# A bf16-bit exponential on VectorE for 60 of 1024 score banks, and GpSimd's weight copies and key masks removed

## The chip, the cores and the metric

The kernel runs on one core of one Trainium2 chip. The metric is the device time of one execution in microseconds (us), as a median of executions; lower is better. A trace of one execution is taken by the hardware profiler. Its span, from the first instruction to the last, is about 2 us shorter than the reported time of the same execution. Each execution also has a mean granted TensorE clock (1.0 is full); below I call an execution *clean* when that is 0.997 or more.

## The reference, cut to what matters

Two attention branches over 2048 positions, 16 heads of 28, joined at the end:

```python
def _A_ref(x, wq, wk, wv, wo):            # 16 query heads, one key/value head
    q = (x @ wq).reshape(B, S, H, Dh)...; k = x @ wk; v = x @ wv
    scores = einsum("bhqd,bkd->bhqk", q, k) * Dh ** -0.5
    p = softmax(scores); o = einsum("bhqk,bkd->bhqd", p, v)
    return o... @ wo
def _B_ref(x, wqkv, wo):                  # each position sees itself and 7 earlier ones, 2 apart
    ...
return concatenate([a, b], axis=-1)
```

Branch A dominates: 16 x 2048 x 2048 exponentials. The kernel handles them as 1024 *banks* of 128 keys x 512 queries.

## The kernel before

All work is listed as operations with an engine, a modelled duration, dependencies and a priority. A small list scheduler in the kernel file then lays out one fixed order for each engine. That matters for reading every experiment: *any* edit that changes a duration, a dependency or a priority gives a new order on all engines.

The main loop takes five banks a round, in PSUM slots of three and of two banks. TensorE computes scores (QK), ScalarE takes the exponential of a whole slot into one of seven ring buffers, TensorE multiplies by V (PV) in groups of four banks. In 51 rounds the third bank of a slot goes to VectorE instead (`off`). A "quad" is 64 banks, four heads of one query block, whose PV sums share a PSUM bank.

```python
ERING = 7
OFF_EVERY, OFF_FROM, OFF_TO = 6, 28, 396
...
x = a("act", t_exp(w), lambda e, b0=b0, w=w, n=n: e.activation(
    g.expT[:, n % ERING, 0:w], g.ps[:, 512 * b0:512 * b0 + w], ACT.Exp, scale=SCALE), ...)
for i in range(na):
    where.append((us[i], ("expT", n % ERING), g.expT[:, n % ERING, 512 * i:512 * i + 512], 0))
if off:
    where.append((us[na],) + g.d_exp(b0 + na, slot) + (1,))
while len(where) >= 4 or (where and pos == NU):
    grp, where = where[:4], where[4:]          # a PV group: four banks in the order of the keys
    ...
def d_exp(self, bank, slot):                   # VectorE's recipe: five instructions of 512 elements
    a("dve", ..., ii = max(bank * A2 * F, -127 * F))        # PSUM -> int32
    a("dve", ..., ee = (hi + 127.0) * 128.0)                # exponent bits, int16
    a("dve", ..., uu = (lo + EP * F) * lo)                  # a cubic of the fraction
    a("dve", ..., vv = (lo + ER * F) * ee.bitcast(BF16))
    a("dve", ..., out = (uu + EQ * F * F) * vv)             # bf16
```

(The five calls are shortened to their arithmetic; cuts are marked by dots.) Branch B's matrix products, softmax and weighted sums run beside this, in 16 blocks, mostly on VectorE and on PSUM banks of their own.

## Time and profile before

| | before |
|---|---|
| time, median of 4 executions | 482.71 us (482.48 to 486.05) |
| span of the profiled execution (485.64 us) | 483.8 us |
| ScalarE / VectorE / GpSimd busy | 457.4 / 378.6 / 40.7 us |
| banks on ScalarE / VectorE | 973 / 51 |
| first exponential starts, last ends | 12.27, 474.78 us |

The profiled execution was one of the slower ones; the prediction, which quotes the lines of its profile, argued that from the head's clock.

### The profile page before, as it was taken

To read this page: it belongs to the slowest core of one execution; us is meant where nothing else is said; L and a number is where in the kernel's file an instruction comes from. 1 tells how busy PE (TensorE), PEld (TensorE's weight loads), DVE (VectorE), ACT (ScalarE), POOL (GpSimd) and SP (SyncE) were. 2 spreads that over 40 slices of the span, in tenths; PEclk is the share of its full clock that TensorE was granted. 3 is DMA by queue.
4 is the path that set the end of the run, shared out by engine and by line. 5 is a ranking of instruction groups with operands and counts; after the bars stand their busy time and mean duration, and the time that the engine had idled before them with its cause. 6 is when DMAs were issued, how large, how long until landed. Compare 5 with 4: busy or idle time off the path is not lost.

```text
span 483.8 us, 8734 instructions
## 1 busy us (share of the span) xinstructions
PE 456.6 (94%) x3630; PEld 177.3 (37%) x3630; DVE 378.6 (78%) x703; ACT 457.4 (95%) x431; POOL 40.7 (8%) x71
## 2 busy tenths in 40 slices
PE   8999999999999999999999999998999999998886
PEld 3333343333343443433333333433334343333333
DVE  4325787998869888889878988788968989888673
ACT  3789999999999999999999998999999999999993
POOL 8643000000000000000000000000000000000000
PEclk9699999999999999999999999999999999999999
DMA  7890202020200320002020320002300330102001
GB/s 160 146 230 14 88 11 76 11 77 10 87 11 20 106 80 26 11 1 82 6 95 11 110 85 27 11 11 71 102 11 2 105 105 20 58 30 96 1 1 57
DMA packets 42071, 27.34 MB, mean 57 GB/s; under 512 B 17090, under 2 KB 41968, under 8 KB 42032
## 3 DMA queue, kind: packets, MB, share of 16 engines
q1 hardware_dynamic: 40080, 25.65, 18.5%
q10 hardware_dynamic: 1776, 0.81, 0.7%
q8 instruction: 28, 0.46, 0.4%
q0 software_dynamic: 176, 0.33, 0.2%
q14 instruction: 11, 0.09, 0.1%
HBM read 17.60 MB, written 5.52 MB: 48 GB/s over the span
## 4 chain that ended last, share of the span: by engine, by line
ACT 62%; PE 35%; DVE 1%; DMA 1%; ACTq 0%; issue 0%; DVEq 0%
ACT expT L756 62%; PE ps L740 7%; PE ps L902 6%; PE ps L770 6%; PE ps L738 4%; PE ps L688 2%; PE ps L918 2%; PE ps L830 1%; PE ps L1014 1%; PE ps L615 1%; DMA d_i<-in_A_wq_dram 1%; PE ps L651 1%; PE ps L861 1%; PE ps L1007 1%; PE ps L702 0%; PE ps L380 0%
## 5 line engine op out<-in xcount | busy, mean ns | idle before, releaser
L756 ACT ACTIVATE expT<-ps 128x1024 bf16<-128x1024 f32 (+1 forms) x410 | 450.2, 1223 | 11.6 <-PE ps L740 6.2
L740 PE MATMUL ps<-qT,kT 32*128 32x512 bf16 x734 | 111.3, 388 | 12.4 <-ACT expT L756 9.7
L770 PE MATMUL ps<-expT,v_aug 128*32 128x512 bf16 x973 | 98.7, 393 | 0.1
L738 PE MATMUL ps<-qT,kz 128*128 128x512 bf16 x290 | 84.5, 384 | 8.8 <-ACT expT L756 6.9
L740 PEld LDWEIGHTS ps<-qT,kT 32*128 32x128 bf16 x734 | 27.2, 91 | 82.1 <-ACT expT L756 58.4
L770 PEld LDWEIGHTS ps<-expT,v_aug 128*32 128x32 bf16 x973 | 24.1, 93 | 63.6 <-issue 57.8
L943 DVE TENSOR_TENSOR stage<-qTB,kTB 112x1024 bf16<-112x1024 bf16 x64 | 44.0, 706 | 4.0 <-PE ps L952 4.0
L802 DVE TENSOR_SCALAR d_i<-ps 128x512 int32<-128x512 f32 x51 | 35.3, 692 | 14.3 <-PE ps L740 13.1
L838 POOL COPY rrep<-rden 128x512 bf16<-128x512 bf16 x15 | 12.7, 843 | 399.4 <-DVE rden L836 399.4
L902 PE MATMUL ps<-xT_B,wqkv 128*112 128x512 bf16 (+1 forms) x128 | 43.2, 405 | 0.2 <-DVE qT L711 0.2
L996 DVE TENSOR_TENSOR prod<-Vsh,a_n 128x896 bf16<-128x896 bf16 x64 | 38.1, 626 | 0.0
L807 DVE SCALAR_TENSOR_TENSOR d_u<-d_i 128x512 f32<-128x512 uint16 x51 | 36.0, 706 | 0.0
L809 DVE SCALAR_TENSOR_TENSOR d_v<-d_i,d_e 128x512 f32<-128x512 uint16 x51 | 35.2, 690 | 0.0
L812 DVE SCALAR_TENSOR_TENSOR dexp<-d_u,d_v 128x512 bf16<-128x512 f32 x51 | 34.8, 682 | 0.0
L738 PEld LDWEIGHTS ps<-qT,kz 128*128 128x128 bf16 x290 | 19.3, 99 | 35.2 <-ACT expT L756 28.3
L952 PEld LDWEIGHTS ps<-ones,stage 112*128 112x128 bf16 x512 | 20.9, 96 | 13.4 <-issue 7.9
L952 PE MATMUL ps<-ones,stage 112*128 112x4 bf16 x512 | 25.2, 167 | 0.2 <-DVE qT L711 0.2
L1007 PE MATMUL ps<-ident,padd 128*112 128x128 bf16 x256 | 25.1, 226 | 0.0
L1007 PEld LDWEIGHTS ps<-ident,padd 128*112 128x112 bf16 x256 | 18.9, 129 | 12.3 <-issue 9.4
L902 PEld LDWEIGHTS ps<-xT_B,wqkv 128*112 128x112 bf16 (+1 forms) x128 | 14.3, 127 | 22.1 <-issue 17.2
L805 DVE TENSOR_SCALAR d_e<-d_i 128x512 int16<-128x512 int16 x51 | 21.6, 423 | 0.2
L830 PEld LDWEIGHTS ps<-sel,PV_sb 128*128 128x128 f32 x128 | 18.9, 190 | 5.5 <-issue 3.9
(109 smaller groups left out, 441.3 us busy)
## 6 DMA issues: line engine op xcount, KB each, us to landing
Vsh<-v_scratch SPq DMA_DIRECT2D x16, 896.0 KB, 4.6
v_scratch<-Vst SPq DMA_DIRECT2D x16, 112.0 KB, 1.7
out_dram<-outB SPq DMA_DIRECT2D x16, 112.0 KB, 1.7
out_dram<-outA SPq DMA_DIRECT2D x14, 112.0 KB, 1.8
wqkv<-in_B_wqkv_dram SPq DMA_DIRECT2D x1, 672.0 KB, 4.8
stage<-in_A_x_dram ACTq DMA_DIRECT2D x1, 448.0 KB, 3.5
wo_B<-in_B_wo_dram SPq DMA_DIRECT2D x4, 98.0 KB
wo<-in_A_wo_dram SPq DMA_DIRECT2D x4, 98.0 KB
```

The source lines that it names most:

```text
L738: r = e.matmul(g.bank(b0 + i), g.kz[:, j, 128 * tb:128 * tb + 128], g.qT[:, sc % 2, t, :], start=True, stop=True)
L740: r = e.matmul(g.bank(b0 + i), g.kT[32 * j:32 * j + 32, 128 * tb:128 * tb + 128], g.qT[32 * j:32 * j + 32, sc % 2, t, :], start=True, stop ...
L756: x = a("act", t_exp(w), lambda e, b0=b0, w=w, n=n: e.activation(g.expT[:, n % ERING, 0:w], g.ps[:, 512 * b0:512 * b0 + w], ACT.Exp, scale ...
L770: x = e.matmul(g.bank(PVBANK, p0=32 * j, p1=32 * j + 32), g.v_aug[:, w, tb, :], src, start=tb == 0, stop=tb == 15, tile_position=(0, 32 * j))
L802: a("dve", t_dve_ps(512), lambda e: e.tensor_scalar(out=ii, in0=g.bank(bank), scalar1=A2 * F, scalar2=-127 * F, op0=ALU.mult, op1=ALU.max) ...
L807: a("dve", t_dve_1x(512), lambda e: e.scalar_tensor_tensor(out=uu, in0=lo, scalar=EP * F, in1=lo, op0=ALU.add, op1=ALU.mult), R=[("d_i", h ...
L809: a("dve", t_dve_1x(512), lambda e: e.scalar_tensor_tensor(out=vv, in0=lo, scalar=ER * F, in1=ee.bitcast(BF16), op0=ALU.add, op1=ALU.mult) ...
L902: a("pe", t_mm(512), lambda e, u=u, t=t, kt=kt, w=w: e.matmul(g.bank(u.bank, p1=KC), g.wqkv[64 * (kt // 3):, kt, w * D + KC * t:w * D + KC ...
L943: op = a("dve", t_dve_2x(1024), lambda e, t=t, qv=qv, kv=kv: e.tensor_tensor(out=g.prodT[0:KC, t, :, :], in0=qv, in1=kv, op=ALU.mult), R=R ...
L952: r = e.matmul(g.bank(u.bank, 128).rearrange("p (h w) -> p h w", w=WIN)[:, 4 * t:4 * t + 4, w], g.prodT[0:KC, t, w, :], g.ones4[:, :], sta ...
L996: a("dve", t_dve_2x(2 * D), lambda e, qr=qr, Vv=Vv, av=av: e.tensor_tensor(out=g.prod2[:, 2 * qr:2 * qr + 2, :].rearrange("p w (d h) -> p ...
L1007: a("pe", 0.09, lambda e, u=u, t=t, w=w: e.matmul(g.bank(u.bank, 128, 128 * t, p1=KC), g.padd[:, w, KC * t:KC * t + KC], g.ident[:, :], st ...
```

## The change

The intent: take nine more banks from ScalarE with a cheaper VectorE recipe that works directly on the bits of bf16, and remove GpSimd's weight copies and key masks. Around it, PV groups, softmax layout, head and pace of branch B are rearranged. The scheduler's model changes too: durations marked `Lock` are VectorE operations that the model makes longer while GpSimd works, and the other way round. The diff, cut to its core:

```diff
-OFF_EVERY, OFF_FROM, OFF_TO = 6, 28, 396
-DR = 4
+OFF_AT = {q: (0, 2, 5, 7) for q in range(1, 16)}      # rounds of each quad, 4 x 15 = 60 banks
+DR = 2
...
-            g.kz_ops[c] = [a("gp", 0.8, ...
+            g.kz_ops[c] = [a("dve", Lock(0.29), ...           # masks of the keys
...
-        u = Use(f"V{c}", g.LB)
+        u = Use(f"V{c}", g.LB, spare=160)                     # dummy matmuls beside the narrow V ones
...
+                quads[us[i][:2]][us[i][3]].append((us[i], ("expT", n % ERING), ...))
             if off:
-                where.append((us[na],) + g.d_exp(b0 + na, slot) + (1,))
+                dunits.append((us[na],) + g.d_exp(b0 + na, slot))
+                if len(dunits) == 4:
+                    g.pv_group(dunits, 1)                      # VectorE's banks: a PV group of their own
...
 def d_exp(self, bank, slot):
+            out=xx[...], in0=g.bank(bank), scalar1=-128.0 * A2, scalar2=128.0 * (129 + EOFF), mult, add   # PSUM -> fp32
+        if h:                                                  # once for two banks, 1024 elements
+                out=u, in0=lo, scalar=EP * F, in1=lo, op0=ALU.add, op1=ALU.mult
+                out=v, in0=u, scalar=EQ * F * F, in1=lo, op0=ALU.add, op1=ALU.mult
+                out=out, in0=v, scalar=EL / F ** 3, in1=xx, op0=ALU.mult, op1=ALU.subtract   # int16 = bf16 bits
...
-    B0 = 34.0
-    BSTEP = 25.0
+    B0 = 32.0
+    BSTEP = 24.5
...
-        self.e_t = sb([128, 2, 2, H, WIN], FP32, "e_t")
+        self.e_t = sb([128, 2, 2, WIN, H], FP32, "e_t")
-        a("act", t_act(256), lambda e: e.activation(fl(g.e_t), fl(g.lg2), ACT.Exp, scale=SCALE),
+        a("act", t_act(256), lambda e: e.activation(ew, g.lg2[:, par], ACT.Exp, scale=SCALE),    # writes 64 bytes apart
-                out=g.a_n[:, par, b].rearrange("p w h -> p h w"), in0=g.e_t[:, par, b],
+                out=g.a_n[:, par, b], in0=g.e_t[:, par, b],
```

GpSimd's four copies that permuted the V weights go too: the eviction of V permutes instead, and the weights have their own buffer and an early load.

## The prediction

> **What bounds the kernel now.** I read the page first: busy shares, the slices, the chain, the costliest groups. ScalarE is 95% busy and its slices read 9 from the third to the last but one; the chain that ended last is ScalarE's exponentials for 62% of the span and TensorE for 35%.
>
> ```profile
> span 483.8 us, 8734 instructions
> PE 456.6 (94%) x3630; PEld 177.3 (37%) x3630; DVE 378.6 (78%) x703; ACT 457.4 (95%) x431; POOL 40.7 (8%) x71
> ACT  3789999999999999999999998999999999999993
> PEclk9699999999999999999999999999999999999999
> ACT 62%; PE 35%; DVE 1%; DMA 1%; ACTq 0%; issue 0%; DVEq 0%
> ```
>
> TensorE's 94% is pipelined matmuls plus dummy ones; VectorE at 78% has room. So the kernel is a ScalarE stream with a head and a tail. The groups by shape size that stream, and the VectorE rows show what one offloaded bank costs now:
>
> ```profile
> L756 ACT ACTIVATE expT<-ps 128x1024 bf16<-128x1024 f32 x255 | 258.9, 1065 | 4.9 <-PE ps L770 3.2 <-PE ps L740 1.0 <-PE ps L738 0.2
> L756 ACT ACTIVATE expT<-ps 128x1536 bf16<-128x1536 f32 x154 | 229.2, 1488 | 6.7 <-PE ps L740 5.1 <-PE ps L738 0.9
> ...
> L807 DVE SCALAR_TENSOR_TENSOR d_u<-d_i 128x512 f32<-128x512 uint16 x51 | 36.0, 706 | 0.0
> L802 DVE TENSOR_SCALAR d_i<-ps 128x512 int32<-128x512 f32 x51 | 35.3, 692 | 14.3 <-PE ps L740 13.1 <-PE ps L738 0.7
> L809 DVE SCALAR_TENSOR_TENSOR d_v<-d_i,d_e 128x512 f32<-128x512 uint16 x51 | 35.2, 690 | 0.0
> L812 DVE SCALAR_TENSOR_TENSOR dexp<-d_u,d_v 128x512 bf16<-128x512 f32 x51 | 34.8, 682 | 0.0
> ...
> L805 DVE TENSOR_SCALAR d_e<-d_i 128x512 int16<-128x512 int16 x51 | 21.6, 423 | 0.2
> ...
> L983 DVE TENSOR_TENSOR a_n<-e_t,rs 128x128 bf16<-128x128 f32 x16 | 11.4, 757 | 0.1
> ```
>
> The reader is to see that 51 banks are already off ScalarE (154 x 3 + 255 x 2 + 1 = 973 of 1024 remain), and that in the whole run ScalarE waited only 4.9 + 6.7 = 11.6 us ahead of its exponentials. The timeline of ScalarE says where: the first exponential starts at 12.27 us, the last ends at 474.78. Of the 11.6 us, 0.5 is the first start, about 3.4 us fall between 17 and 33 us, 3.2 us are three stalls at 126, 187 and 295 us, and the rest is crumbs of 0.2 to 0.4 us. The three stalls:
>
> ```profile
> 126.15 25.49 ACT L756 ACTIVATE expT<-ps 128x1024 bf16<-128x1024 f32 x23 [1.04 <-PE ps L770]
> 187.35 11.12 ACT L756 ACTIVATE expT<-ps 128x1024 bf16<-128x1024 f32 x10 [0.54 <-PE ps L770]
> 295.22 16.66 ACT L756 ACTIVATE expT<-ps 128x1024 bf16<-128x1024 f32 x15 [1.62 <-PE ps L770]
> ```
>
> At each, the PV group that should free a buffer of the exponential ring contains one VectorE-made bank: at 293.52 us the last step of that bank begins, 0.68 us long, and the PV group follows at 294.77, while ScalarE is out of ring buffers. The stall of the head is the clock. In 2 us windows:
>
> ```profile
> 14.00:16.00 2.00, 2.00 (x17) 0.76 (x14) 1.18 (x2) 2.00 (x3) 0.94 (x2) 1.00 0.62 111
> 16.00:18.00 2.00, 2.00 (x18) 0.93 (x17) 1.06 (x5) 1.59 (x3) 1.68 (x5) 0.54 0.52 101
> 24.00:26.00 2.00, 2.00 (x13) 0.29 (x13) 0.26 (x1) 1.42 (x1) 1.70 (x4) 0.50 0.98 205
> ```
>
> The third number from the right is the granted clock: half from about 17 to 26 us, right after the narrow V matmuls (28 columns) of 12.6 to 14 us.
>
> **What the Trainium skill says.** (1) "ScalarE: Activation LUTs", section "What ACT_TABLE_LOAD costs": 0.833 ns an element, and back-to-back activations overlap by about 93 ns. The trace agrees: (1488 - 1065) / 512 = 0.826 ns, and the durations, about 488.7 us with the one 512 wide, exceed the busy 450.2 by 38.5 us, 94 ns each for 410. So a bank is worth 0.423 us of ScalarE, whatever its neighbours. (2) "VectorE: DVE Perf Modes", section "The TRN2 errata — SBUF-src ops pay a fixed extra latency per instruction": fp32 two-tensor operations take (N + 151) / 0.96 ns, 691 at 512; the trace's 706, 690 and 682 agree, and at 1024 it gives 1224. (3) "Advanced Engine Details and Errata", section "SBUF Cachelines": accesses that each fall in another 16-byte line are penalised. The trace has one case that fits: a_n writes bf16 32 bytes apart and takes 757 ns, while the subtraction of the same 128 x 128, written densely, takes 283. (4) "TensorE: Matmul & The Clock Gate", section "What's actually happening": too little TensorE activity in a window of about 3.4 us halves the clock, and the window runs freely, so the phase differs by run. That fits the half clock above, and perhaps the spread of the three times, 482.48 and 482.72 against 486.05.
>
> **The change part by part.**
> 1. *Nine more banks on VectorE.* Four in each of 15 quads give 60 instead of 51. The count of exponentials stays 410, but 60 - 51 = 9 shrink from 1536 to 1024: 9 x 0.423 = 3.8 us less ScalarE, all on the bounding stream. Minus 3.8.
> 2. *The VectorE recipe.* Before: 692 + 423 + 706 + 690 + 682 = 3193 ns a bank, 51 banks, 162.8 us. After, a pair of banks: two PSUM reads of 692 and three operations of 1024 elements at 1224, so 5056 ns, 30 pairs, 151.7 us. VectorE does nine more banks in 11 us less. Off the path: worth nothing directly, but it lowers the delay of PSUM evacuations.
> 3. *a_n made dense*, 16 x (757 - 283) = 7.6 us less VectorE, off the path. The price is in ScalarE's softmax exponential of branch B, which now writes fp32 64 bytes apart. If it pays what a_n paid per element, (757 - 283) / 128 = 3.7 ns, that is 256 x 3.7 = 0.95 us more on each of 8 calls, 7.6 us on the bounding engine. If ScalarE pays nothing, 0. No row of before shows ScalarE writing with a stride; I choose 2 us as an estimate between. Plus 2.0.
> 4. *PV groups separated.* Banks of VectorE get PV groups of their own, so no group that frees ring buffers contains one. The 3.2 us of stalls lose their cause; but the groups now take their four columns from different key blocks, which holds some ring buffers about 1.6 exponentials longer of 7, and TensorE, in order, can still stand before an early VectorE group. I take 2.5 us off and put 1.0 us back for new waits. Minus 1.5.
> 5. *GpSimd.* Its four weight copies (about 0.95 us each, at 38 to 42 us) and 16 kz masks (706 ns each) go; the masks take about 0.28 us each on VectorE (the 448-element copy of the same kind took 280 ns), 4.5 us in a head where VectorE is a third busy or less. The V eviction now permutes in its PSUM read: possibly longer than 621 ns, not on the path. Zero.
> 6. *Head.* Dummy matmuls beside the narrow V ones should keep the clock. In this trace the half clock cost some 3 us, but the two fast executions are 3 us below the profiled one (485.64), so I hold that the median of 482.72 does not contain it. The gain is in the spread, zero on the median. The added V-weight load on GpSimd's queue competes with the transposed loads; chunk 1 is needed only after 6 or 7 exponentials. Zero.
> 7. *Tail.* Branch B starts 2 us earlier and steps 24.5 instead of 25 us, 9.5 us earlier at its last block. In the tail VectorE's eviction for B (0.69 us from 478.11) pushes the last normalisation from about 478.4 to 478.71, and B's store is issued last. Minus 0.4.
>
> Sum: 482.7 - 3.8 + 2.0 - 1.5 - 0.4 = 479.0. I shade this to 478.5 because lighter VectorE load should also shave some crumbs of waiting.
>
> **The rivals.** *A floor.* Between first start and last end (462.5 us) ScalarE idles 11.1 us; without idle and with 3.8 us less it needs 447.6. With a head of 12.3 and a tail of 9.0 the span is 468.9; the profiled run's time was 1.84 us over its span, so about 470.7 is the least. A gain of over 2% (below 473.1) needs nearly all waiting gone and no stride penalty. For it: the stalls have nameable causes, and the change addresses two. Against it: a static order always leaves crumbs. I give such a result 472 us. *ScalarE's strided write eats the gain.* For it: a_n's 757 ns. Against: that was a 2-byte write on another engine. Full penalty: 482.7 - 3.8 + 7.6 - 1.9 = 484.6, "within 2%". *VectorE's longer instructions become the bound.* A PSUM read that finds a 1.22 us operation just begun frees its bank up to 0.5 us later than now, and a short exponential gives only 0.97 us. Against: the read goes first in the order, the rounds 0, 2, 5, 7 leave the three long operations to rounds without offload, and VectorE's total falls. If a quarter of 60 reads cost 0.4 us: plus 6, 485. *TensorE stalls on an early VectorE PV group*: one stall of 1 us in each quad would be plus 15, 494; the priorities make it improbable.
>
> **Range and chances.** The sum's spread is mainly the stride (0 to 7.6), the waits (-5 to +5) and the clock's phase (3): 473.5 to 484.0, predicted 478.5. Faster by over 2% needs the floor nearly reached: 0.08. Slower by over 2% (above 492.4) needs a new stall per quad: 0.03. Within 2%: 0.89.
>
> **What would show it right or wrong.** Exponentials 145 x 1536 and 264 x 1024 with unchanged means (step 1); three VectorE operations near 1.22 us, 30 times each, and VectorE near 365 us busy (2); the mean of the B softmax exponential against 455 ns, and a_n near 283 ns (3); waits of exponentials for PV gone or below 1 us (4); clock full from 12 to 30 us (6); last exponential to end below 9 us (7). I am wrong if ScalarE's idle ahead of exponentials rises above 11.6 us, or B's exponential is over 1 us, or the head moves by more than 1 us from 12.27.

## The result, and the profile after

| | before | after |
|---|---|---|
| time, median of 4 executions | 482.71 us | 478.56 us (478.50 to 478.89) |
| ratio | | 0.9899, 95% interval 0.9856 to 0.9943 |

The change is faster by 1.0%, inside the band of 2% that the prediction gave most of its chances. Ratios here are the mean time of one kernel's runs over that of the other's runs of the same rounds; so they are not quite the ratio of the medians. Executions over 1.5% slower than the fastest of the same kernel are left out of the means. The 486.05 of before counts in that mean, though its clock was lost for a while. The page of the changed kernel, first busy times, then two slices and the chain:

```profile
span 476.5 us, 8559 instructions
PE 451.4 (95%) x3605; PEld 178.3 (37%) x3605; DVE 375.6 (79%) x614; ACT 454.6 (95%) x431; POOL 29.4 (6%) x45
ACT  3899999999999999999999999999999999999993
PEclk9999999999999999999999999999999999999999
ACT 65%; PE 31%; SPq 1%; DMA 1%; DVE 1%; issue 0%; DVEq 0%
```

Nothing has changed places: ScalarE still reads 9 nearly throughout, and VectorE is almost as busy as before (375.6 against 378.6), although it does nine more banks. The groups of the changed kernel (instructions, shapes, count, then busy us and mean ns, then idle ahead of them and its releasers):

```profile
L766 ACT ACTIVATE expT<-ps 128x1024 bf16<-128x1024 f32 x264 | 264.9, 1047 | 2.7 <-PE ps L750 2.0 <-PE ps L748 0.4
L766 ACT ACTIVATE expT<-ps 128x1536 bf16<-128x1536 f32 x145 | 213.3, 1471 | 4.5 <-PE ps L750 2.5 <-PE ps L748 1.4
L1001 ACT ACTIVATE e_t<-lg 128x256 f32<-128x256 f32 x8 | 5.2, 648 | 0.0
...
L823 DVE TENSOR_SCALAR d_x<-ps 128x512 f32<-128x512 f32 x60 | 41.4, 689 | 11.3 <-PE ps L750 7.4 <-PE ps L748 2.6
L830 DVE SCALAR_TENSOR_TENSOR d_u<-d_x 128x1024 f32<-128x1024 uint16 x30 | 36.5, 1217 | 0.1
L834 DVE SCALAR_TENSOR_TENSOR dexp<-d_u,d_x 128x1024 int16<-128x1024 f32 x30 | 36.4, 1214 | 0.1
L832 DVE SCALAR_TENSOR_TENSOR d_u<-d_u,d_x 128x1024 f32<-128x1024 f32 x30 | 36.3, 1211 | 0.1
L645 DVE TENSOR_SCALAR kz<-kT,cols 128x512 bf16<-128x512 bf16 x16 | 6.3, 391 | 0.4
L1007 DVE TENSOR_TENSOR a_n<-e_t,rs 128x128 bf16<-128x128 f32 x16 | 4.1, 285 | 0.1
```

The counts are 145 and 264 as planned. Releasers named "L770", the PV matmuls that cost 3.2 us of ScalarE before, have no counterpart here (PV is now L790, and it does not appear). The price of the layout is in the third row: 648 ns where 455 stood.

To compare like with like, I ran the kernel before once more.

### x0_before: the kernel before again, for a trace at full clock

No edit.

> The kernel before, unedited, once more for a second trace. Theory (the profiled execution of before had a half clock from 17 to 26 us that its faster executions did not have): if this execution takes about 482.7 us, its trace shows full clock from 12 to 40 us and about 8 us of ScalarE idle ahead of exponentials instead of 11.6; if it takes about 486, the half clock is there again. Rival (the half clock is in every execution, and the 3 us come from elsewhere): half clock at 482.7 us too.

It took 482.63 us, correct. Its trace, the same two windows as in the prediction (third number from the right: clock) and its exponentials:

```profile
16.00:18.00 2.00, 2.00 (x22) 1.10 (x20) 1.40 (x5) 2.00 (x4) 1.68 (x4) 1.00 0.43 89
24.00:26.00 2.00, 2.00 (x20) 0.90 (x20) 0.00 (x0) 2.00 (x4) 0.95 (x2) 1.00 1.14 233
```

```profile
L756 ACT ACTIVATE expT<-ps 128x1024 bf16<-128x1024 f32 x255 | 259.0, 1066 | 4.6 <-PE ps L770 3.2 <-PE ps L740 0.8 <-PE ps L738 0.2
L756 ACT ACTIVATE expT<-ps 128x1536 bf16<-128x1536 f32 x154 | 229.2, 1489 | 4.1 <-PE ps L740 2.5 <-PE ps L738 0.9
```

The clock is full, the idle is 4.6 + 4.1 = 8.7 instead of 11.6 us, and the span is 480.8. So the half clock of the first trace belongs to the slower executions. The three stalls on PV stand unchanged: they belong to the order, not to the clock.

Now the 4.3 us between the spans 480.8 and 476.5 can be split. First exponential: 12.60 against 12.67, nothing. From there to the end of the last: 459.1 against 455.1, minus 4.0. Tail: 9.1 against 8.8, minus 0.3. Within the stretch, all exponentials together occupy 449.7 us of ScalarE before (450.2 in the trace with the half clock) and 446.1 after, minus 3.6; the softmax of B costs 3.6 and 5.2, plus 1.6; the waits inside the stretch (8.7 less 0.5 at the first start, 7.2 less 0.8) fall by 1.8. That is minus 3.8, within a few tenths of the 4.0: records of ScalarE overlap, so such sums are good to that.

### The profile page after: what moved, and what is told of

It is laid out like the page before. It is cut to its first block, busy times and chain, and to the rows that moved or that the text cites.

```text
span 476.5 us, 8559 instructions
## 1 busy us (share of the span) xinstructions
PE 451.4 (95%) x3605; PEld 178.3 (37%) x3605; DVE 375.6 (79%) x614; ACT 454.6 (95%) x431; POOL 29.4 (6%) x45
## 4 chain that ended last, share of the span: by engine, by line
ACT 65%; PE 31%; SPq 1%; DMA 1%; DVE 1%; issue 0%; DVEq 0%
ACT expT L766 64%; PE ps L750 7%; PE ps L924 6%; PE ps L790 5%; PE ps L748 4%; PE ps L852 2%; PE ps L696 2%; PE ps L940 1%; SPq L560 1%; DMA xT_A<-in_A_x_dram 1%; PE ps L883 1%; PE ps L1038 1%; PE ps L660 1%; PE ps L392 1%; ACT e_t L1001 0%
## 5 line engine op out<-in xcount | busy, mean ns | idle before, releaser
L766 ACT ACTIVATE expT<-ps 128x1024 bf16<-128x1024 f32 (+1 forms) x410 | 446.1, 1196 | 7.2 <-PE ps L750 4.5
L748 PE MATMUL ps<-qT,kz 128*128 128x512 bf16 x305 | 88.1, 382 | 9.6 <-ACT expT L766 7.5
L790 PE MATMUL ps<-expT,v_aug 128*32 128x512 bf16 x964 | 95.7, 389 | 0.4
L823 DVE TENSOR_SCALAR d_x<-ps 128x512 f32<-128x512 f32 x60 | 41.4, 689 | 11.3 <-PE ps L750 7.4
L790 PEld LDWEIGHTS ps<-expT,v_aug 128*32 128x32 bf16 x964 | 24.4, 92 | 66.3 <-issue 62.3
L860 POOL COPY rrep<-rden 128x512 bf16<-128x512 bf16 x15 | 16.8, 1122 | 393.8 <-DVE rden L858 393.8
L830 DVE SCALAR_TENSOR_TENSOR d_u<-d_x 128x1024 f32<-128x1024 uint16 x30 | 36.5, 1217 | 0.1
L834 DVE SCALAR_TENSOR_TENSOR dexp<-d_u,d_x 128x1024 int16<-128x1024 f32 x30 | 36.4, 1214 | 0.1
L832 DVE SCALAR_TENSOR_TENSOR d_u<-d_u,d_x 128x1024 f32<-128x1024 f32 x30 | 36.3, 1211 | 0.1
L1031 PE MATMUL ps<-ident,prod 128*112 128x128 bf16 x256 | 25.6, 226 | 0.0
L1031 PEld LDWEIGHTS ps<-ident,prod 128*112 128x112 bf16 x256 | 19.3, 129 | 12.1 <-issue 8.6
L696 PE MATMUL ps<-xT_A,wq 128*128 128x512 bf16 x64 | 20.5, 384 | 0.5 <-DVE v_aug L675 0.3
```

Of the source, the lines that this page charges most:

```text
L748: r = e.matmul(g.bank(b0 + i), g.kz[:, j, 128 * tb:128 * tb + 128], g.qT[:, sc % 2, t, :], start=True, stop=True)
L790: x = e.matmul(g.bank(PVBANK, p0=32 * j, p1=32 * j + 32), g.v_aug[:, w, tb, :], src, start=first, stop=last, tile_position=(0, 32 * j))
L823: a("dve", t_dve_ps(512), lambda e: e.tensor_scalar(out=xx[:, 512 * h:512 * h + 512], in0=g.bank(bank), scalar1=-128.0 * A2, scalar2=128.0 ...
L830: a("dve", t_dve_1x(1024), lambda e: e.scalar_tensor_tensor(out=u, in0=lo, scalar=EP * F, in1=lo, op0=ALU.add, op1=ALU.mult), R=di, W=["d_ ...
L834: a("dve", t_dve_1x(1024), lambda e: e.scalar_tensor_tensor(out=out, in0=v, scalar=EL / F ** 3, in1=xx, op0=ALU.mult, op1=ALU.subtract), R ...
L1031: a("pe", 0.09, lambda e, u=u, t=t, w=w: e.matmul(g.bank(u.bank, 128, 128 * t, p1=KC), g.padd[:, w, KC * t:KC * t + KC], g.ident[:, :], st ...
```

## The experiments

All executions, in us. Numbers in brackets count clean executions. The runs were taken in three groups on three chips; the medians of the kernel before in them were 482.81, 482.70 and 482.77, so runs of different groups may be compared to about 0.2 us.

| run | median | clean executions | ratio to before |
|---|---|---|---|
| changed kernel, first | 478.56 | 478.50 to 478.89 (4 of 4) | 0.9899 |
| a_again, the same | 479.16 | 478.59 to 479.47 (4 of 6) | 0.9914 |
| e1_dense | 478.60 | 477.85 to 478.67 (4 of 6) | 0.9893 |
| e2_48 | 483.80 | 482.70 (1 of 4) | 1.0021 |
| e3_nofill | 480.17 | 478.90, 478.97 (2 of 6) | 0.9944 |
| e6_oldrecipe | 503.87 | none (6) | 1.0404 |
| e7_mixed | 505.06 | none (7) | 1.0431 |
| e8_64 | 480.69 | 480.14 to 481.70 (5 of 6) | 0.9942 |
| e9_old48 | 485.04 | 484.99 to 485.06 (3 of 4) | 1.0036 |
| e12_mixed48 | 501.73 | 500.89, 502.10 (2 of 4) | 1.0400 |
| e10_oldlayout | 477.83 | 477.64 to 478.25 (5 of 6) | 0.9888 |
| e11_bstep | 480.15 | 479.44 to 480.35 (4 of 6) | 0.9951 |

All gave correct results.

### a_again: the control

No edit.

> The changed kernel unedited, as a control for this group of runs. Every theory: fast executions 478.5 to 478.9 as before; the question is only how often the clock is lost (0 of 4 executions so far, against 3 of 11 above 486 for the kernel before on this chip).

Clean executions as before, but two of six lost the clock (486.16 at clock 0.981, 483.60 at 0.985). On the same chip the kernel before lost it in 4 of 11 (485.86 to 486.47, all at 0.989). So the changed kernel is not immune. With its four first executions that is 2 of 10 against 8 of 33 over the three groups of runs: no difference can be claimed.

### e3_nofill: without the dummy matmuls of the head

```diff
-        u = Use(f"V{c}", g.LB, spare=160)
+        u = Use(f"V{c}", g.LB)
```

> The changed kernel without the dummy matmuls beside the narrow V matmuls of the head. Theory (they only keep the clock, whose loss depends on the phase of the execution): most executions about 478.6, some 3 us longer, and a half clock between 16 and 28 us only in the long ones. Rival A (without them every execution loses the clock): all about 481.5. Rival B (they do nothing): all within 0.5 us of 478.6, full clock.

The two clean executions are 0.3 us above the changed kernel's typical time; the other four are 1 to 6 us longer than these, at clocks of 0.982 to 0.996. In the profiled one (479.75 us) the clock was full from 10 to 32 us. It was lost at the other end, in the window of the tail:

```profile
470.00:478.00 8.00, 3.65 (x26) 1.80 (x22) 2.59 (x6) 1.64 (x3) 0.00 (x0) 0.76 0.18 57
```

That loss does not explain this execution's time: its tail (from the last exponential to the end) took 8.4 us, less than the 8.8 of the changed kernel, while its first exponential started 1.1 us later (13.73 against 12.67) at full clock. Other traces end on a half clock too, x0_before for example from 479.6 us on. So neither the theory nor rival A is confirmed; for the clock of the head, this one trace looks like rival B (they do nothing). Since the edit re-laid the whole order, whether the dummy matmuls protect the head stays open.

### e2_48: fewer banks, and e8_64: more

```diff
-OFF_AT = {q: (0, 2, 5, 7) for q in range(1, 16)}
+OFF_AT = {q: (0, 2, 5, 7) for q in range(1, 13)}                                  # e2_48
+OFF_AT = {q: (0, 2, 5, 7) if q else (4, 6, 9, 11) for q in range(16)}             # e8_64
```

> The changed kernel with 12 quads offloaded instead of 15: 48 banks instead of 60. Theory (a bank is worth 0.423 us of the bounding ScalarE): 12 x 0.423 = 5.1 us slower, 483.6. Rival (part of the worth of a bank is lost in waits caused by VectorE's reads and its own PV groups): under 3.5 us slower, at most 482, with ScalarE's idle smaller than 7.2 us.

> The changed kernel with the first quad offloaded too, its rounds 4, 6, 9 and 11: 64 banks. Theory (each bank is worth 0.423 us of ScalarE, less a sixth lost in waits as in the run with 48 banks, where 12 banks made 4.2 us at full clock): 1.4 us below the changed kernel, 477.1. Rival (VectorE or TensorE is loaded in the first quad, with the transposes and projections of the head): no gain, 478.6 or more, with more idle in ScalarE between 17 and 40 us.

With 48 banks the only clean execution took 482.70, some 4.0 us above the control's middle of 478.7. That is 4.0 / 12 = 0.33 us a bank: between the theory's 0.423 and its rival, and from a single clean execution. The profiled execution (484.32, not clean) agrees: its first exponential came 1.5 us later (14.21), but from there to the end of the last, at full clock, it took 459.4 us against 455.1, which is 0.36 a bank. So a bank is worth most of its ScalarE time, not all. Note that 48 banks with the rest of the change take the 482.7 that 51 took before.

With 64 banks the four additional ones made it *slower*, 480.4 against 478.7. The rival holds. ScalarE's own timeline of that run shows where (in brackets at the end: idle ahead of the row and what ended it):

```profile
36.10 5.37 ACT L766 ACTIVATE expT<-ps 128x1024 bf16<-128x1024 f32 x5 [2.00 <-PE ps L750]
...
44.15 9.34 ACT L766 ACTIVATE expT<-ps 128x1024 bf16<-128x1024 f32 x9 [1.26 <-PE ps L790]
```

Two new stalls, 2.00 and 1.26 us, in or just after the first quad, where head work still runs on TensorE and VectorE, outweigh 4 x 0.423 = 1.7. In the changed kernel no stall between 30 and 50 us is longer than 0.27. It fits that the change leaves that quad out.

### e1_dense: the strided write of ScalarE undone

```diff
-        self.e_t = sb([128, 2, 2, WIN, H], FP32, "e_t")
+        self.e_t = sb([128, 2, 2, H, WIN], FP32, "e_t")
-        ew = g.e_t[:, par].rearrange("p b w h -> p b h w")
+        ew = g.e_t[:, par]
-                out=g.a_n[:, par, b], in0=g.e_t[:, par, b],
+                out=g.a_n[:, par, b], in0=g.e_t[:, par, b].rearrange("p h w -> p w h"),
```

The modelled durations are untouched, and the orders of all engines are row for row the same as in the changed kernel (55 records of matmuls are missing from this trace, as they are from a_again's), which makes this the cleanest of the comparisons.

> The changed kernel with branch B's exponential writing densely again, and the normalisation reading it with a stride instead and still writing densely. Theory (the strided fp32 write costs ScalarE 648 - 455 = 0.19 us in each of 8 calls, all on the bounding engine): that exponential back to about 455 ns, total 477.0, 1.5 us below the changed kernel; normalisation on VectorE between 285 and 757 ns, without effect on the total. Rival (the 0.19 us hide in waits): no change, 478.5.

```profile
L766 ACT ACTIVATE expT<-ps 128x1024 bf16<-128x1024 f32 x264 | 265.4, 1049 | 3.0 <-PE ps L750 2.0 <-PE ps L748 0.7
L766 ACT ACTIVATE expT<-ps 128x1536 bf16<-128x1536 f32 x145 | 213.5, 1472 | 5.0 <-PE ps L750 2.9 <-PE ps L748 1.7
L1001 ACT ACTIVATE e_t<-lg 128x256 f32<-128x256 f32 x8 | 3.4, 427 | 0.0
```

The write is back to 427 ns, 8 x (648 - 427) = 1.8 us less. The clean executions gained only about 0.4 (median 478.36 against the control's 478.8; the two ranges overlap). The traces show where the rest went. ScalarE's busy time fell by 1.0 only (454.6 to 453.6), since its records overlap their neighbours. Between the first exponential and the end of the last, the waits ahead of exponentials rose by 0.5 (6.4 to 6.9), and the stretch became 0.6 shorter (455.1 to 454.5). So part of the saving was overlapped before and part is spent waiting for the next scores: the rival is nearer the truth, and "on the bounding engine" does not mean "one for one in the time".

### e6_oldrecipe and e9_old48: the old recipe on the new frame

The five-instruction recipe of before replaces the new one in the changed kernel; the buffers and the constant of the second V weights follow.

```diff
-        xx, out = g.d_x[:, m % 2, :], g.dexp[:, m % DR, :]      # two banks, then three operations of 1024
...
+        h = m % 2                                               # d_exp as in the kernel before
...
+OFF_AT = {q: (0, 2, 5, 7) for q in range(1, 13)}                # e9_old48 in addition
```

> The changed kernel with the old VectorE recipe (five instructions of 512 elements for each bank) on the new 60 banks, with the new PV groups. Theory (VectorE is not the bound, so its cheaper recipe is worth nothing directly): within 0.7 us of the changed kernel, VectorE some 10 us busier. Rival (the recipe's saving is what lets VectorE keep up with 60 banks): over 2 us slower, with more ScalarE idle ahead of exponentials than 7.2 us.

> The old VectorE recipe with new PV groups, at 48 banks instead of 60. Theory (60 banks at 3.19 us each overfilled VectorE, and branch B finished about 25 us late; 48 banks do not overfill it): the last output eviction of branch B returns from 498.7 us to before 480, total 482.7 to 485, within 1.5 us of the run with 48 banks and the new recipe. Rival (the old recipe is slow for another reason, such as its short instructions breaking up the others): more than 5 us above that run.

With 60 banks: 503.87, 25 us slower. This is the largest surprise. VectorE's share on the page is still modest:

```profile
PE 459.5 (92%) x3604; PEld 183.9 (37%) x3658; DVE 403.0 (80%) x764; ACT 456.3 (91%) x431; POOL 24.8 (5%) x45
```

But the exponentials are not what ends late: in e6 the last one is done at 469.2, and ScalarE's idle ahead of them is 7.5 us against 7.2, so the rival's total came, but not by way of ScalarE. Branch B is late. The row of branch B's output evictions (min/median/max ns, then first and last start in us), for the kernel before (the trace of x0_before), the changed one, e6 and e9:

```profile
L1017 DVE CAST outB<-ps x16: 610/624/626, 115.9 to 477.6; 128x448 bf16<-128x448 f32 x16
```

```profile
L1041 DVE CAST outB<-ps x16: 616/625/626, 113.3 to 473.4; 128x448 bf16<-128x448 f32 x16
```

```profile
L1042 DVE CAST outB<-ps x16: 623/625/626, 135.4 to 498.7; 128x448 bf16<-128x448 f32 x16
```

```profile
L1042 DVE CAST outB<-ps x16: 614/625/626, 135.8 to 480.2; 128x448 bf16<-128x448 f32 x16
```

In e6 the first block of B is evicted 22 us later than in the changed kernel and the seventh 60 us later (334.6 against 274.5 us), and the last starts 25 us later. The run with 48 banks has the same times as e6 up to the tenth block (397 against 404), and then, when its last quads offload nothing, catches up: last eviction at 480.2, total 485.0. That is 2.3 us above the 48-bank run with the new recipe, more than the 1.5 I allowed and far less than the rival's 5. My reading: VectorE's time per quad is short. In windows of 100 us between 50 and 350 us it is busy for 81 to 89 us in all these kernels (82 to 86 in the changed one, 84 to 88 in e6), and part of what is left are waits that a fixed order does not fill. The old recipe's 3.19 us a bank, 28.7 us more for nine banks, does not fit in time for branch B; the new recipe's does. That the recipe costs 25 us in the schedule made for it is shown. How much of it is sheer time, and how much a worse order that the scheduler laid out, I did not separate, so the cause is in part argued.

### e7_mixed and e12_mixed48: PV groups that mix both kinds of banks

```diff
-                dunits.append((us[na],) + g.d_exp(b0 + na, slot))
-                if len(dunits) == 4:
-                    g.pv_group(dunits, 1)
...
+                dunits.append((us[i], ("expT", n % ERING), ..., 0))      # ScalarE's banks join the same list
...
+                dunits.append((us[na],) + g.d_exp(b0 + na, slot) + (1,))
+            while len(dunits) >= 4:                 # groups of four in the order of the keys
+                g.pv_group(dunits[:4])
```

on top of e6 and of e9.

> The same as the run with the old recipe, but PV groups formed in the order of the keys again, so that a group that frees exponential buffers may contain one VectorE bank. Theory (these mixed groups cause the stalls of 1.04, 0.54 and 1.62 us of the kernel before): ScalarE's idle that ends on a PV matmul comes back, 2 to 4 us, and the total is 1.5 to 4 us above the run with separated groups. Rival (the stalls were accidents of one order): idle on PV matmuls below 0.5 us and totals within 0.7 us.

> The old recipe at 48 banks with PV groups in the order of the keys, which may contain a VectorE bank. With branch B no longer last, theory: the waits of exponentials for PV matmuls (19.3 us in the mixed run with 60 banks) stay at 8 us or more and now show in the total, at least 5 us above the separated run with 48 banks. Rival (the stalls fill slack that would be lost anyway): within 2 us of it.

With 60 banks the stalls came back, and larger. The wait list of ScalarE in e7 (us in total, times, longest), where e6 has no such row:

```profile
ACT expT L767 <- PE ps L787: 19.3, 12, 3.8
```

That is far more than the 2 to 4 us expected. The total hardly moved (505.06 against 503.87), below the 1.5 us expected, because branch B ended last in both. With 48 banks, where B is not far behind, the same row of 19.3 us stands in e12's trace, and it shows in the time: 500.89 at full clock against 485.02, 15.9 us. This confirms the mechanism: a PV group that waits for VectorE holds the exponential ring, and separating the groups removes that. (Going back to the order of the keys also changes which ring buffers a group frees; the two were not undone apart.) It was worth little in the kernel before, whose own placement lost only 3.2 us to it, and much under the new placement.

### e10_oldlayout: the whole softmax layout undone

```diff
-        self.e_t = sb([128, 2, 2, WIN, H], FP32, "e_t")
+        self.e_t = sb([128, 2, 2, H, WIN], FP32, "e_t")
-        a("act", t_act(256), lambda e: e.activation(ew, g.lg2[:, par], ACT.Exp, scale=SCALE),
+        a("act", t_act(256), lambda e: e.activation(fl(g.e_t), fl(g.lg2), ACT.Exp, scale=SCALE),
-            a("dve", 0.32, lambda e, b=b: e.tensor_tensor(
-                out=g.a_n[:, par, b], in0=g.e_t[:, par, b],
+            a("dve", 0.62, lambda e, b=b: e.tensor_tensor(
+                out=g.a_n[:, par, b].rearrange("p w h -> p h w"), in0=g.e_t[:, par, b],
```

> The changed kernel with the softmax of branch B laid out as before: dense exponential on ScalarE (455 instead of 648 ns), normalisation on VectorE writing with a stride (about 757 instead of 285 ns), 7.5 us more VectorE work less 1.3 us in the sum. Theory (VectorE is at its edge in the changed kernel, branch B's last eviction at 473.4 us comes after the last exponential at 467.8): the last eviction of B is 4 to 7 us later and the total 1 to 5 us higher, 480 to 484. Rival (VectorE has room, its work is off the path, as the prediction had it): 477.0 to 478.6.

My theory fell. VectorE's normalisation took 773 ns again and VectorE 380.8 us in all, 5.2 more, and the time went *down*, to 477.83; its five fast executions (477.64 to 478.25) all lie below every one of the changed kernel's (478.50 and more). B's last eviction came earlier, not later:

```profile
L1040 DVE CAST outB<-ps x16: 615/625/626, 115.9 to 464.6; 128x448 bf16<-128x448 f32 x16
```

So VectorE has room for 5 us, though not for e6's 27 (403.0 - 375.6). The old layout is worth about 0.9 us here (477.83 against 478.7); some of it may be the new order. This version beats both kernels, by little.

### e11_bstep: branch B at its old pace

```diff
-    B0 = 32.0
-    BSTEP = 24.5
+    B0 = 34.0
+    BSTEP = 25.0
```

> The changed kernel with branch B started at 34 and paced at 25 us as before, instead of 32 and 24.5. The prediction's step: only the tail feels it, 0.4 us later, 478.9. Theory of now (branch B's progress is set by VectorE's free time, so its last eviction moves less than the 9.5 us of the plan): last eviction of B later by 0 to 5 us, total 478.6 to 482. Rival (the pace is what brought B in before the end): last eviction about 9 us later, total 485 or more.

Clean executions at 479.9, about 1.2 us slower; the last eviction of B was *earlier*, at 460.2. So the eviction's time is not the measure that I took it for, and the predicted 9.5 us shift does not exist. The tail was 8.6 us (last exponential until 470.35 of a span of 479.0). In this trace (480.98, not clean) the first exponential started 1.0 us later than in the changed kernel, and the stretch from there to the end of the last was 1.6 us longer, 1.0 of it waits (7.4 against 6.4). So the pace acted through the order of the middle, not through the tail.

## Why the prediction was right, point by point

The predicted 478.5 met 478.56. The main term had the right sign and size, and the errors of the others were small or cancelled: the banks were worth 0.5 to 0.8 us less than predicted, and the strided write cost 1 us or more less. That the total came out within 0.1 us, in a stated range of 473.5 to 484.0, is luck. The last 0.5 us, taken off for lighter VectorE load, has no support: VectorE's busy time fell by 3 us only, and 5 us more of it did no harm (e10).

1. *Nine more banks.* Counts exact. Predicted minus 3.8 of ScalarE; the exponentials occupy 3.6 us less. In the time, e2_48 gives 0.33 to 0.36 us a bank, 3.0 to 3.3 for nine. The means were said to stay and fell by 17 and 18 ns. And the prediction misread the overlap of neighbouring records: 488.7 us was a sum of the rows' busy times, in which overlaps inside a row are already taken out, and not of durations. Durations (count times mean, and 0.6 for the one exponential of 512) give (271.6 + 229.2 + 0.6 - 450.2) / 410 = 125 ns before and (276.4 + 213.3 + 0.6 - 446.1) / 410 = 108 ns after. The records became shorter and overlap less by the same amount: 1065 - 125 = 940 and 1047 - 108 = 939 ns for an exponential of two banks. So the pace stayed, and the 0.423 us, which is a difference of means, is not touched.
2. *The recipe.* The step that failed: "Off the path: worth nothing directly". The durations were right (1217, 1211 and 1214 ns against 1224). But without the cheaper recipe 60 banks cost 25 us in the order that the scheduler laid out (e6), so it is what pays for the nine banks; at 48 banks its lack cost 2.3 us (e9). I had read VectorE's 78% as room; in the middle it is 82 to 86%, and the rest is usable only in part: 5 us of it at no cost (e10), not 27. The predicted 365 us busy was 375.6: I multiplied mean durations by counts, but VectorE's records overlap as ScalarE's do (about 80 ns where no wait lies between, as at 74.10 us, 0.28 us long, followed at 74.30), so the many short instructions removed had cost less busy time than their sum: durations fell by 13 us (423.7 to 410.1), the busy time by 3.
3. *a_n and the strided write.* Direction right, size of the term off: 0.19 us a call instead of the 0.25 chosen, 1.5 us raw; undoing it gained about 0.4 (e1) to 0.9 us (e10, with the new order), not the 2.0 of the sum. a_n became 285 ns, as predicted.
4. *PV groups.* Right: waits on PV 3.2 us to none, waits inside the stretch minus 1.8 against the predicted minus 1.5; the mechanism is shown by e12 against e9, for a placement in which it costs far more than before.
5. *GpSimd.* Zero for the total, in agreement with the sum, though no run isolates it. The masks took 391 ns each on VectorE, not 280; V's permuting eviction stayed at 621.
6. *Head.* Right that the median of before holds no half clock (x0_before). "The gain is in the spread" is not supported: the changed kernel lost its clock in 2 of 10.
7. *Tail.* Minus 0.3 was measured against minus 0.4, but not by the step's mechanism: B's last eviction is still in the tail (473.4 of 476.5), and the slower pace did not lengthen the tail (e11).

Of the rivals, the floor was not approached: 7.2 us of waiting remain. The full stride penalty did not come, nor did late PSUM reads by long VectorE operations: in the list of TensorE's waits in the changed kernel no row ends on VectorE's read of a score bank.

## What to carry to other kernels

When two engines share a load, price the second one too: an offload is free only until the other engine's leftover work ends last, and in e6 that happened at a busy share of 80%. An instruction shortened on the busiest engine may return only in part (1.8 us of records gave about 0.4 us in e1), so undo one part at a time on the chip. And before comparing traces, get one of each kernel in the same clock.

## What the Trainium skill lacked or had wrong

- "Advanced Engine Details and Errata", section "SBUF Cachelines", names a penalty but no size. The "Vector Engine (DVE) Microarchitecture Reference", section "Measured stream behaviour on trn2 (trn3 not measured)", has sizes for VectorE on 4-byte words alone, so those for ScalarE and for 2-byte writes are lacking. Here: ScalarE writing 256 fp32 64 bytes apart 648 instead of 455 ns, 0.75 ns an element; VectorE writing 128 bf16 32 bytes apart 757 instead of 285 ns, 3.7 ns an element; VectorE reading 256 fp32 64 bytes apart in a sum 572 instead of 414 ns, 0.6 ns an element. So a strided 2-byte write by VectorE cost five to six times as much an element as the other two.
- "ScalarE: Activation LUTs", section "What ACT_TABLE_LOAD costs", gives about 93 ns for the overlap of back-to-back activations. Averaged over all 410 exponentials it is more here: 125 ns before and 108 after.
- No page read gives the cost of a per-partition scalar on VectorE. Evictions of 128 x 512 from PSUM took 749 ns with one (adding a column) and 689 without (the same kind of instruction with two constants, d_x).
- "SBUF — State Buffer", section "Who interferes with whom", says a GpSimd instruction that reads SBUF contends with a VectorE one with two SBUF inputs. GpSimd's copies of the reciprocals, whose form did not change, went from a mean of 846 to 1122 ns (longest 1500) when VectorE's two-input operations became 1.2 us long; with the old recipe's 0.7 us operations in the new kernel (e6) the mean was 814 and the longest 947. That agrees, so nothing is lacking there; the copies are off the path in both kernels.
